# DeltaNet and an MLP in one kernel: chunk 0's inverse on four quadrants, and an instruction order worked back from deadlines

## The chip, the cores and the metric

The kernel runs on one core of a Trainium2 chip. The metric is the device time of one execution in microseconds; before the change it is 635.73 us, the median of three runs (632.64 to 637.24). The profiled execution has a span of 635.3 us. TensorE (PE) multiplies, VectorE (DVE), ScalarE (ACT) and GpSimd (POOL) do elementwise work, and SyncE (SP), ScalarE and GpSimd issue transfers.

## What is computed

There are 4 batches of 8 heads, 768 positions, head dimension 48. The attention is a delta rule with a state per head:

```
state = 0                                   # (48, 48) for each batch and head
for t in range(768):
    y[t]  = q[t] @ state
    v_old = k_n[t] @ state                  # k_n = k / (|k| + 1e-6)
    state = state + beta[t] * outer(k_n[t], v[t] - v_old)
```

The heads are put side by side to rows of 384, and a feed-forward block follows on each row:

```
xn  = (x - mean) / sqrt(var + 1e-6) * g_ln
out = x + relu(xn @ w_ch1) @ w_ch2          # 384 -> 1536 -> 384
```

All data is float32.

## The kernel before

**Chunks.** The 768 positions are cut into 12 chunks of 64 (C = 64). Within a chunk the recurrence is a triangular system: the matrix G holds the products of keys with each other, scaled by beta and the norms; X is the inverse of the unit triangular matrix; U = X (v - K S) gives the updates; the output is y = Q S + (masked Q K) U; and the state becomes S + K^T U. `recur(c)` holds these steps, layer norm and the transposes to the MLP's input `xnt`; `mlp(c)` holds the 12 first-layer steps (L1238, one for each 128 hidden columns, each three matmuls of 128x256) and 2 x 12 second-layer steps (L1254, 128x384 each) of a chunk's 256 rows. A matmul of float32 shows as two records in the profile. 32 (batch, head) pairs are stacked as two halves of 64 partitions (`half(e)`, e = 0 or 1) by 16 heads on the free axis; `GH` is 16, and groups g = 0 and 1 of 8 heads each are treated in turn.

**Three ways to the inverse.** From chunk 2 on, two chunks at a time form a slab: `prep_g` makes their G, stores it to DRAM and reloads it so that each partition has one 32x32 block, `rows_inverse` inverts it in 31 steps of two VectorE operations (L973, L978), the blocks go back through DRAM, and `join` puts the 64x64 inverse together with products E (L1037) and Z (L1042). Chunk 1 does the same with 16x16 blocks, 15 steps and two joins. Chunk 0 can't wait so long: `first_inverse` doubles the inverse on TensorE in levels n = 1 to 5. A level masks G (L816, on VectorE for n = 1 and 2, on GpSimd otherwise), multiplies it with the transposed inverse so far (E, L835), copies the result (L838), multiplies with a widened copy of the inverse (Z, L857 and L855), and writes back the inverse (L872) and its transpose (L873); `widen` (L807) makes the copy with both 32-column blocks. In these products both operands and the result of head (e, h) lie in the same half e. Only the tiles at rows 0, columns 0 and rows 64, columns 64 of the array are used. In the other attention products (`recur`, `products` for queries) odd heads have their result in the other half: `e ^ hp`, with hp the parity of the head, so all four 64x64 tiles work in turn.

**Weights.** w_ch1 and w_ch2 arrive as 12 pieces of 768 KB (`fetch`) into five buffers, two of which lie in `h_all`, and are converted with two ScalarE, three VectorE and one GpSimd operation a piece (`convert`: L633, L638, L643, L648, L653, L665).

**What sets the order.** Nothing runs in the order of the program text. Every operation is recorded as a `Step` with an engine, an assumed cost, its dependences and a priority `pr`; `Line.run` plays these forward with its own assumed times and picks, on each engine, the ready step with the lowest `pr`. `Line.emit` then issues all steps in that order, and `in_this_order` pins it, so each engine works through a fixed list. In the kernel before, `pr` was written by hand: -100 for chunk 0's chain, 10 c and nearby for chunk c, 1000 + 10 c for MLP steps, which thus fill gaps. `hold` steps (those at -100 and less) make an engine wait for them a little rather than start something long.

Of the kernel before, what the change touches and what calls it, by code (L numbers as in the profile page):

```python
# [16 lines left out]
C = 64  # L17
# [42 lines left out]
class Step:  # L60
    __slots__ = (
        "eng", "cost", "fn", "deps", "pr", "lag", "bulk", "start", "end", "n", "users", "name", "t0", "np", "arr", "hold", "ready"
# [3 lines left out]
class Line:  # L66
# [3 lines left out]
    HOP, GIVE = 0.17, 0.1  # L70
    PE_TAIL = 0.12
# [9 lines left out]
    def add(self, eng, cost, fn, r=(), w=(), pr=0.0, lag=0.0, bulk=None, name="", t0=0.7, after=(), np=0, arr=0.0, hold=None):  # L81
        s = Step()
        s.eng, s.cost, s.fn, s.pr, s.lag, s.bulk, s.name, s.t0 = eng, cost, fn, pr, lag, bulk, name, t0
        s.np, s.arr, s.n = np, arr, len(self.steps)
        s.hold = pr <= -100 if hold is None else hold
        deps = set()
        for k in r:
            if k in self.writer:
                deps.add(self.writer[k])
        for k in (*w, *after):  # L90
            if k in self.writer:
                deps.add(self.writer[k])
            deps.update(self.readers.get(k, ()))
        for k in r:
            self.readers.setdefault(k, []).append(s)
        for k in w:
            self.writer[k] = s
            self.readers[k] = []
        deps.discard(s)
        s.deps = sorted(deps, key=lambda d: d.n)  # L100
        s.start = s.end = None
        self.steps.append(s)
        return s
# [6 lines left out]
    def pe_time(self, s, t, commit):  # L110
        passes, bi, begun, wins = self.passes, self.block, self.begun, self.wins
        left, stall, new = max(s.np, 1), 0.0, {}
# [20 lines left out]
        if commit:  # L133
            self.passes, self.block, self.begun = passes, bi, begun
# [48 lines left out]
    def foresee(self, now):  # L183

        soon, ends = {e: [] for e in ENGS}, {}
        for s in self.held:
# [4 lines left out]
            t = max(s.t0, now)  # L191
# [7 lines left out]
    def run(self):  # L199
# [3 lines left out]
        self.passes, self.block, self.begun, self.wins = 0, 0, 0.7, {}  # L203
        self.avail = {e: [] for e in ENGS}
# [19 lines left out]
        while todo:  # L224
# [26 lines left out]
            if e == "PE" and len(now) > 1 and pick.pr >= 0 and pick.pr < 900:  # L251
                z, stall = self.pe_time(pick, t, False)
                if stall > 0.25:
                    for s in now:
                        if s.pr >= 900 and self.pe_time(s, t, False)[1] < 0.05:
                            pick = s
                            break
            first = [r for r, h in self.soon[e] if h.start is None and h.pr < pick.pr and t < r]
            if first and t + pick.cost > first[0] + self.GIVE and waits.get(e, 0) < 4:
# [3 lines left out]
                else:  # L263
                    waits[e] = waits.get(e, 0) + 1
# [28 lines left out]
    def schedule(self):  # L293
# [4 lines left out]
        for s in self.steps:  # L298
            s.users = users[s]
        self.run()  # L300
# [7 lines left out]
def kernel(  # L308
# [81 lines left out]
    bm = [sb(f"bm{i}", [128, 2]) for i in range(2)]  # L390
# [13 lines left out]
    dsw = sb("dsw", [128, GH])  # L404
# [52 lines left out]
    c_dve(lambda: nc.vector.memset(nought[:, 0:640], 0.0), 0.45, [("esx", 0), ("esx", 1)], pr=-300)  # L457
# [16 lines left out]
    for i in range(2):  # L474
        for b in range(2):
            c_dve(
                lambda i=i, b=b: nc.vector.tensor_scalar(
                    out=bm[i][:, b : b + 1], in0=xb[:, 0, 0:1].bitcast(I32), scalar1=b ^ i, scalar2=None, op0=ALU.is_equal
                ),
                0.15, [("bm", i, b)], ["bma"], pr=-99,  # L480
            )
# [16 lines left out]
    MPR = [-200, -99, -98, -98, -98, -98, -30]  # L498
    for n in range(7):
# [20 lines left out]
    MASK_SCRATCH = [(x, n) for x in ("ma", "mb") for n in range(7)] + ["bma", "eyx"]  # L520
    xc = us.rearrange("p h d -> p (h d)")[:, 0 : GH * BK].rearrange("p (h t) -> p h t", t=BK)
    c_pool(
        lambda: nc.gpsimd.tensor_copy(out=xc, in_=eye[:, None, :].to_broadcast([128, GH, BK])),
        0.62, [("xc", 0), ("xc", 1)], ["eye"],
# [20 lines left out]
    def load_first(engs, **kw):  # L545
        for g in range(2):
            for e in range(2):
                dma(
                    engs[e], tb[0].rearrange("p (h d) -> p h d", d=DP)[half(e), g * H : g * H + H, 0:D],
                    k[2 * e + g, :, 0:C, :].rearrange("h p d -> p h d"), H * C, 16.5, [], [("tb", 0, e, g)], **kw,  # L550
                )
# [22 lines left out]
    def load_blocks(i, src, c, eng, **kw):  # L574
        dst = tb[i].rearrange("p (h u d) -> p h u d", u=2, d=BK)
        for hp in range(2):
            for m in range(2):
                w = min(BK, D - BK * m)
                p0 = DP * hp + BK * m
                for u in range(2):  # L580
# [5 lines left out]
                        after=[("tb", i, e, g) for e in range(2) for g in range(2)], **kw,  # L586
                    )

    def tb_keys(i, kind):
# [3 lines left out]
        return [("tb", i, e, kind) for e in range(2)] + [("tbpad", i)]  # L593


    ON_DVE = (1, 2)
    BIG, SMALL, LEV = 2, 0, 0
# [78 lines left out]
    def fill(n, cols, size=128, behind=None, **kw):  # L676

        def go():
            for _ in range(n):
                nc.tensor.matmul(ffb[0:size, 1, 0:cols], nought[0:size, 512 : 512 + size], nought[0:size, 0:cols])  # L680
        t = max(PASS, cols * 0.845e-3) * 2 * n
        f = add("PE", t, go, [("esx", 0), ("esx", 1)], [FF2[0]], np=2 * n, arr=2 * n * cols * 0.845e-3 * (size / 128) ** 2, name="fill", **kw)
        if behind:
            f.deps.append(behind)
# [17 lines left out]
    def first_beta(ps, pk, **kw):  # L702
        def turn():
            for e in range(2):
                nc.tensor.matmul(ps[half(e), 0:GH], brow[BK * e : BK * e + GH, 0:C], ident[BK * e : BK * e + GH, BK * e : BK * e + GH])
        add("PE", 0.1, turn, [("brow", e) for e in range(2)] + ["ident"], pk, np=4, arr=0.02, **kw)
        add("DVE", 0.2, lambda: nc.vector.tensor_copy(out=bnat, in_=ps[:, 0:GH]), pk, ["bnat"], **kw)
# [21 lines left out]
    def first_swaps(**kw):  # L729
        add("ACT", 0.22, lambda: nc.scalar.mul(dsw[:, 0::2], ndb[:, 0::2], -1.0), [("nd", 0), ("nd", 1)], [("ds", 0)], **kw)  # L730
        for e in range(2):
            add(
                "ACT", 0.22, lambda e=e: nc.scalar.mul(dsw[half(1 - e), 1::2], ndb[half(e), 1::2], -1.0),
                [("nd", 0), ("nd", 1)], [("ds", 1 + e)], **kw,
# [24 lines left out]
    GM = [None, (gsbs[2], "g", 2), (gsbs[3], "g", 3), (xts[2], "xt", 2), (xts[3], "xt", 3), (gsbs[2], "g", 2)]  # L759
# [5 lines left out]
    def first_inverse(p_gk, gk, p_e, ek, p_x, xk, fill=None, **kw):  # L765

        gs, xt = gsbs[0], xts[0]
        pe_ = p_e.rearrange("p n (h t) -> p n h t", t=BK)
        px = [p_x[:, g, 0 : H * BK].rearrange("p (h t) -> p h t", t=BK) for g in range(2)]
        p_g = p_gk.rearrange("p n (j t) -> p n j t", t=C)  # L770
        shape = [128, H, 2, BK]
        kw0 = kw
        for g in range(2):
# [11 lines left out]
            for b in range(2):  # L785
# [4 lines left out]
                        xc[:, s], masks[0][:, None, cols].to_broadcast([128, H, BK]), gs[:, s, cols]  # L790
                    ),
                    [("g", 0, g), ("mask", 0)], [("xc", g)], **kw,
                )
            add("DVE", 0.45, lambda s=s: nc.vector.transpose(xnj[:, s], xc[:, s]), [("xc", g)], [("xn", g)], **kw)
            pe(
                2, lambda s=s, g=g: nc.tensor.matmul(px[g], ident, xnj[:, s], start=True, stop=True, skip_group_check=True),
                ["ident", ("xn", g)], xk[g], 0.43, **kw,
            )
# [3 lines left out]
        def widen(g):  # L802

            for b in range(2):
                o = spread(xt)[:, heads2[g], b]
                add(
                    "ACT", act(256), lambda o=o, b=b: nc.scalar.mul(o, xc[:, heads2[g]], bm[0][:, b : b + 1]),  # L807
                    [("xc", g), ("bm", 0, b)], [("xt", 0, g, b)], **kw,
                )

        def mask(n, g):
            gm, mk, s = GM[n][0], GM[n][1:], heads2[g]
            eng = ("DVE", nc.vector, dve(512)) if n in ON_DVE else ("Pool", nc.gpsimd, 0.3 + 1.95e-3 * 512)
# [8 lines left out]
        for n in range(1, 6):  # L822
            gm, mk = GM[n][0], GM[n][1:]
            last = n == 5
            for g in range(2):
                mask(n, g)
                if not last:
                    widen(g)
            for g in range(2):
                s = heads2[g]  # L830

                def prod_e(g=g, gm=gm):
                    for h in range(g * H, g * H + H):
                        for e in range(2):
                            nc.tensor.matmul(pe_[half(e), 0, h], gm[half(e), h], xnj[half(e), h])  # L835
                pe(32, prod_e, [mk + (g,), ("xn", g)], [ek[g]], 0.22, name=f"E{n}", **kw)
                if not last:
                    add("ACT", act(256), lambda s=s: nc.scalar.copy(es[:, s], pe_[:, 0, s]), [ek[g]], [("es", g)], **kw)  # L838
                    continue
                add(  # L840
                    "DVE", dve(512),
                    lambda s=s: nc.vector.tensor_tensor(
                        out=spread(esx)[:, s], in0=pe_[:, 0, s, None, :].to_broadcast(shape),
                        in1=bm[1][:, None, :, None].to_broadcast(shape), op=ALU.mult,
                    ),
                    [ek[g]] + [("bm", 1, b) for b in range(2)], [("esx", g)], **kw,
                )
            for g in range(2):
                s = heads2[g]

                def prod_z(g=g, last=last):
                    for h in range(g * H, g * H + H):
                        for e in range(2):
                            if last:
# [563 lines left out]
```

## Time and profile before

| What | Before |
|---|---|
| time, median of three | 635.73 us |
| TensorE busy, share of the span | 583.6 us, 92% |
| VectorE, ScalarE, GpSimd busy | 313.5, 172.0, 123.1 us |
| first product of chunk 0's inverse | 15.9 us |
| U of chunk 0 (second group) | 63.0 us |
| first MLP matmul | 81.1 us |
| first row step of slab 1 | 128.3 us |
| first join product of chunk 2 | 188.2 us |

A line of a timeline has the start, the duration of the group, engine, line, operation, output and inputs, shape and count, and in brackets how long the engine was idle before it and what ended that. A line of busy time by stage has the stretch, its length, busy time and count of instructions of each engine, the mean TensorE clock that was granted, the share of DMA and GB/s.

### The profile page before, as it was taken

To read this page: it belongs to the slowest core of one execution; us is meant where nothing else is said; L and a number is where in the kernel's file an instruction comes from. 1 tells how busy PE (TensorE), PEld (TensorE's weight loads), DVE (VectorE), ACT (ScalarE), POOL (GpSimd) and SP (SyncE) were. 2 spreads that over 40 slices of the span, in tenths; PEclk is the share of its full clock that TensorE was granted. 3 is DMA by queue.
4 is the path that set the end of the run, shared out by engine and by line. 5 is a ranking of instruction groups with operands and counts; after the bars stand their busy time and mean duration, and the time that the engine had idled before them with its cause. 6 is when DMAs were issued, how large, how long until landed. Compare 5 with 4: busy or idle time off the path is not lost.

```text
span 635.3 us, 20372 instructions
## 1 busy us (share of the span) xinstructions
PE 583.6 (92%) x9108; PEld 438.0 (69%) x9108; DVE 313.5 (49%) x711; ACT 172.0 (27%) x395; POOL 123.1 (19%) x163
## 2 busy tenths in 40 slices
PE   7887697568899989999999999999999999999996
PEld 5777675345677766866776867868767767777673
DVE  6345899367802589224784137871339812320000
ACT  5337375011221331223220331302322212222010
POOL 5264653711420224001340000010010100100000
PEclk9555689758799999999999999999999998999999
DMA  9921558873452563315815146103241040010101
GB/s 195 244 42 17 151 175 196 122 111 56 83 100 49 140 92 51 92 28 118 135 23 100 23 120 102 34 35 59 53 103 27 1 92 4 2 26 1 25 1 25
DMA packets 159975, 48.49 MB, mean 76 GB/s; under 512 B 151048, under 2 KB 154256, under 8 KB 159888
## 3 DMA queue, kind: packets, MB, share of 16 engines
q1 hardware_dynamic: 154032, 42.65, 32.6%
q0 software_dynamic: 2720, 3.96, 3.6%
q8 instruction: 71, 1.16, 0.8%
q10 hardware_dynamic: 3136, 0.59, 0.7%
q14 instruction: 16, 0.13, 0.1%
HBM read 33.93 MB, written 13.24 MB: 74 GB/s over the span
## 4 chain that ended last, share of the span: by engine, by line
PE 77%; DVE 9%; ACT 4%; SPq 3%; DMA 3%; issue 2%; DVEq 0%; ACTq 0%
PE ffa L1254 19%; PE ffa L1238 18%; PE ffb L1254 10%; PE ffb L1238 8%; SPq L441 3%; PE by L857 2%; PE two L835 2%; PE ffb L1042 2%; PE ffb L1037 2%; PE two L902 2%; PE two L1157 2%; PE by L1147 2%; PE two L1087 1%; PE by L1208 1%; PE two L1140 1%
## 5 line engine op out<-in xcount | busy, mean ns | idle before, releaser
L1238 PE MATMUL ffa<-xnt,w_sb 128*128 128x256 f32 x600 | 148.6, 394 | 5.8 <-ACT h_all L1246 3.7
L1254 PE MATMUL ffa<-w_sb,h_all 128*128 128x384 f32 x384 | 144.7, 495 | 1.2 <-ACT h_all L1246 1.1
L1238 PEld LDWEIGHTS ffa<-xnt,w_sb 128*128 128x128 f32 x600 | 113.6, 194 | 29.3 <-ACT h_all L1246 8.0
L1254 PEld LDWEIGHTS ffa<-w_sb,h_all 128*128 128x128 f32 x384 | 70.0, 190 | 46.0 <-ACT h_all L1246 4.0
L1254 PE MATMUL ffb<-w_sb,h_all 128*128 128x384 f32 x192 | 82.7, 517 | 5.3 <-DVE xt L1052 2.4
L1246 ACT ACTIVATE h_all<-ffa 128x256 f32<-128x256 f32 x100 | 35.0, 382 | 144.0 <-PE ffa L1238 103.5
L1238 PE MATMUL ffb<-xnt,w_sb 128*128 128x256 f32 x264 | 65.0, 382 | 0.2 <-DVE o L1263 0.2
L978 DVE TENSOR_TENSOR xb<-xb,tmp 128x60 f32<-128x60 f32 (+19 forms) x170 | 61.2, 360 | 5.8
L973 DVE TENSOR_TENSOR tmp<-xb,gb 128x60 f32<-128x60 f32 (+19 forms) x170 | 59.9, 352 | 3.3
L1072 POOL TENSOR_SCALAR knrm<-knrm 128x16 f32<-128x16 f32 x11 | 3.3, 297 | 275.9 <-ACT knrm L1068 275.9
L1238 PEld LDWEIGHTS ffb<-xnt,w_sb 128*128 128x128 f32 x264 | 49.5, 190 | 8.6 <-DVE o L1263 0.3
L1254 PEld LDWEIGHTS ffb<-w_sb,h_all 128*128 128x128 f32 x192 | 35.5, 196 | 28.6 <-DVE xt L1052 4.8
L441 POOL DMA_DIRECT2D tb<-in_k_dram x80 | 52.5, 663 | 11.2 <-DVE kt L886 10.7
L1052 DVE COPY xt<-ffb 32x512 f32<-32x512 f32 x22 | 15.0, 684 | 62.5 <-PE ffb L1037 28.5
L1246 ACT ACTIVATE h_all<-ffb 128x256 f32<-128x256 f32 x44 | 16.9, 384 | 76.7 <-PE ffb L1238 59.1
L1263 DVE TENSOR_TENSOR o<-ffa,x 128x384 f32<-128x384 f32 x16 | 8.7, 555 | 45.0 <-PE ffa L1254 43.7
L1030 DVE STREAM_TRANSPOSE xnj<-xt 128x512 f32<-128x512 f32 x11 | 7.8, 709 | 44.1 <-PE ffb L1037 23.8
L1263 DVE TENSOR_TENSOR o<-ffb,x 128x384 f32<-128x384 f32 x8 | 4.4, 555 | 40.7 <-PE ffb L1254 40.6
L653 POOL TENSOR_TENSOR words<-words,x 128x768 f32<-128x768 f32 (+1 forms) x11 | 20.1, 1828 | 22.7 <-DVE tmp L973 8.5
L1047 ACT ACTIVATE es<-ffb 32x512 f32<-32x512 f32 x22 | 13.0, 589 | 37.8 <-PE ffb L1254 15.2
L1064 DVE TENSOR_REDUCE ksum<-xln 128x16 f32<-128x768 f32 x11 | 10.5, 952 | 23.1 <-ACT xln L1063 23.0
L1181 ACT COPY x<-by 128x384 f32<-128x384 f32 x24 | 10.3, 482 | 36.3 <-PE by L1147 36.3
(161 smaller groups left out, 688.9 us busy)
## 6 DMA issues: line engine op xcount, KB each, us to landing
words<-in_moe_w_ch_dram SPq DMA_DIRECT2D x10, 768.0 KB, 5.2
gd<-gsb SPq DMA_DIRECT2D x11, 512.0 KB, 3.2
v<-in_v_dram SPq DMA_DIRECT2D x24, 192.0 KB, 4.3
kr<-in_k_dram SPq DMA_DIRECT2D x48, 96.0 KB, 3.6
out_dram<-o SPq DMA_DIRECT2D x48, 96.0 KB, 2.2
tb<-in_k_dram POOLq DMA_DIRECT2D x40, 64.0 KB, 3.1
gb<-gd SPq DMA_DIRECT2D x40, 64.0 KB, 3.6
tb<-in_q_dram SPq DMA_DIRECT2D x40, 64.0 KB, 2.8
```

The costliest lines, as they stand in the source:

```text
L441: add(eng, cost, lambda: QUEUE[eng].dma_start(out=out_, in_=in_), r, w, bulk=n * ns / 16e3, **kw)
L653: lambda: nc.gpsimd.tensor_tensor(out=lo.bitcast(FP32), in0=lo.bitcast(FP32), in1=esc.bitcast(FP32), op=ALU.mult),
L835: nc.tensor.matmul(pe_[half(e), 0, h], gm[half(e), h], xnj[half(e), h])
L857: nc.tensor.matmul(px[g][half(e), h - g * H], xt[half(e), h], es[half(e), h], start=False, stop=True, skip_group_check=True,)
L973: nc.vector.tensor_tensor(out=t, in0=xv[:, 0:n, j : j + 1].to_broadcast([128, n, w]), in1=gv[:, j : j + 1, j + 1 : L].to_broadcast([128, n ...
L978: nc.vector.tensor_tensor(out=rest, in0=rest, in1=t, op=ALU.subtract)
L1047: add("ACT", act(512), lambda rows=rows: nc.scalar.mul(es[rows], p[rows], -1.0), [ATT[1]], [("es", e)], **kw)
L1052: "DVE", dve(512), lambda rows=rows: nc.vector.tensor_copy(out=xt[rows, :, BK:C], in_=p[rows]),
L1238: nc.tensor.matmul(p[:, 0:TOK], w1_sb[:, t, f * 128 : (f + 1) * 128], xnt[:, t], start=(t == 0), stop=(t == KC - 1))
L1246: "ACT", act(256), lambda hk=hk, p=p: nc.scalar.activation(h_all[:, hk], p[:, 0:TOK], ACTF.Relu),
L1254: lambda f=f, g=g, p=p, hk=hs[f]: nc.tensor.matmul(p[:, 0:DM], h_all[:, hk, g * 128 : (g + 1) * 128], w2_sb[:, f], start=(f == 0), stop=(f ...
L1263: lambda o=o, p=p, g=g: nc.vector.tensor_tensor(out=o, in0=p[:, 0:DM], in1=x[:, g], op=ALU.add),
```

## The change

It has three parts.

**1. Chunk 0's inverse on four quadrants.** The keys are loaded so that odd heads of half e lie in half 1 - e (`load_first`; 8 loads in place of 4), and E and Z use row half `e ^ hp` and result half e (or the reverse for Z). The running inverse that is one factor of Z must then be in the half of its result, so `odd_back` copies it with three ScalarE operations a group: the even heads straight, the odd heads from one half into the other. E's result goes to the widened factor `esx` directly, one 32-column block on ScalarE (L880) and one on VectorE (L885), so `widen` and one copy a level go. Level 5 is done as in `join`, with 32x32 products (L906, L911). Masks: only level 1 of group 1 stays on VectorE, seven go to GpSimd. The norms move with the odd heads (`knat` in place of `dsw`).

**2. Priorities from deadlines.** Each MLP step gets a `due`: 42.0 + 42.2 c + 1.35 t, less 14 for c > 0. `schedule` goes through the steps backwards and sets `pr` to the latest end that still lets every user keep its own; hand-written priorities no longer count, except that steps nothing waits for get a large one. The steps that the first MLP step needs are laid out alone first, then all together, with the early ones not before their first time (`least`) and the tight ones on `hold`.

**3. Bunching.** On TensorE, once an MLP step is under way, MLP steps go on while one is ready, unless a small step is within 6 (URGENT) of its latest time; and small steps go on once one is under way. The order assumes 0.1 (SWITCH) for each change between the two kinds.

As built, TensorE's list has 153 changes between MLP and other steps where it had 165 (127 and 141 after the first join of chunk 2), 11 second-layer steps of MLP(1) stand before that join where 8 stood, and VectorE's row steps of chunk 1 follow at once on chunk 0's U. Three filler matmuls stand at the start in place of two.

The diff, cut to its core:

```diff
+    HOP, GIVE, PATIENCE, SLACK, EAGER = 0.17, 0.1, 1.5, 3.0, 0.0
+    URGENT, STALL = 6.0, 0.25
+    PE_TAIL, SWITCH = 0.12, 0.1
...
+            if e == "PE":
+                big = [s for s in now if s.due is not None]
+                small = [s for s in now if s.due is None]
+                if big and small:
+                    pick = big[0]
+                    if not self.big or small[0].pr - t < self.URGENT:
+                        fit = [s for s in small if self.pe_time(s, t, False)[1] < self.STALL]
+                        if fit:
+                            pick = fit[0]
+                        elif small[0].pr < t:
+                            pick = small[0]
...
+        for s in reversed(every):
+            took = s.cost if s.bulk is None else s.cost + self.DMA_ISSUE + self.DMA_DONE + 2 * s.bulk
+            took = max(took, 0.031 * s.np if s.due is None else 0.0)
+            late = [u.pr - took - (0.03 if u.eng == s.eng else self.HOP) for u in users[s]]
+            s.pr = min(late + [s.due if s.due is not None else 1e6])
...
+                    engs[e], tb[0].rearrange("p (h d) -> p h d", d=DP)[half(e ^ hp), g * H + hp : g * H + H : 2, 0:D],
+                    k[2 * e + g, hp::2, 0:C, :].rearrange("h p d -> p h d"), NP * C, 16.5, [],
...
-    ON_DVE = (1, 2)
-    BIG, SMALL, LEV = 2, 0, 0
+    ON_DVE = ((1, 1),)
+    BIG = 3
...
+    def odd_back(g, out_, in_, r, w, eng, **kw):
+        s = heads2[g]
+        for n in range(3):
+            hs = slice(s.start + (n > 0), s.stop, 2)
+            po, pi = (slice(0, 128),) * 2 if not n else (half(n - 1), half(2 - n))
+            src = in_[pi, int(n > 0)]
...
-                    for h in range(g * H, g * H + H):
-                        for e in range(2):
-                            nc.tensor.matmul(pe_[half(e), 0, h], gm[half(e), h], xnj[half(e), h])
+                    for h, hp, j, e in order[g]:
+                        a = half(e ^ hp)
+                        nc.tensor.matmul(pe_[half(e), 2 * g, hp, j], gm[a, h], xnj[a, h])
...
+                    for h, hp, j, e in order[g]:
+                        nc.tensor.matmul(
+                            px[g][half(e ^ hp), hp, j], esx[half(e), h], xc[half(e), h],
+                            start=False, stop=True, skip_group_check=True,
+                        )
...
-    first_kt(0, 1, qts[0], ("qt", 0), two, TWO, pr=-94)
-    queries(0, ffb, ATT + FF2, pr=-100)
+    first_kt(0, 1, qts[0], ("qt", 0), ffb, ATT + FF2, pr=-99)
+    queries(0, ffb, ATT + FF2, halves=True, pr=-100)
...
+    def due(c, t):
+        return 42.0 + 42.2 * c + 1.35 * t - (14.0 if c else 0.0)
```

## Prediction

> **What bounds the kernel now.** I read the page's busy line and slices first, then the busy time by stage, then TensorE's and VectorE's timelines of the first 190 us.
>
> ```profile
> PE 583.6 (92%) x9108; PEld 438.0 (69%) x9108; DVE 313.5 (49%) x711; ACT 172.0 (27%) x395; POOL 123.1 (19%) x163
> PE   7887697568899989999999999999999999999996
> PEclk9555689758799999999999999999999998999999
> ```
>
> 92% busy looks finished, but the clock row says otherwise: from slice 13 on TensorE is full at full clock; before it, it is half clocked or waiting. By stage (PE, weight load, DVE, ACT, POOL, clock, DMA):
>
> ```profile
> 0.00:15.90 15.90, 12.28 (x98) 8.31 (x98) 10.24 (x43) 7.98 (x15) 8.14 (x22) 1.00 1.07 195
> 15.90:63.00 47.10, 38.35 (x675) 35.97 (x676) 20.78 (x47) 22.92 (x53) 20.63 (x25) 0.51 0.46 102
> 63.00:81.10 18.10, 12.47 (x367) 11.21 (x367) 15.69 (x26) 6.05 (x12) 11.14 (x11) 0.59 0.52 135
> 81.10:118.20 37.10, 32.50 (x352) 22.70 (x352) 31.64 (x60) 18.95 (x32) 19.81 (x15) 0.94 0.72 177
> 118.20:188.20 70.00, 53.13 (x952) 38.60 (x954) 39.11 (x91) 10.69 (x27) 23.00 (x35) 0.76 0.61 97
> 188.20:635.30 447.10, 434.90 (x6669) 321.16 (x6668) 196.03 (x448) 105.39 (x258) 40.38 (x57) 1.00 0.27 55
> ```
>
> The last row is the bound stage: 434.9 of 447.1 us busy, 5 of the idle 12 us the final store. It can hardly shrink. The 188 us before it hold MLP(0) (31 us when full: 12 x 1.30 + 24 x 0.65 by the starts of L1238 and L1254), two thirds of MLP(1) and attention of two chunks; the rest is lost. Chunk 0's inverse, on TensorE:
>
> ```profile
> 31.96 1.92 PE L835 MATMUL two<-xnj,xt 64*64 64x32 f32 x32 [0.23 <-ACT xnj L872]
> 34.40 3.62 PE L857 MATMUL by<-es,xt 64*64 64x32 f32 x64 [0.52 <-ACT es L838]
> 39.14 3.63 PE L835 MATMUL two<-xnj,xt 64*64 64x32 f32 x64 [1.12 <-ACT xnj L872]
> ...
> 62.99 1.11 PE L1121 MATMUL two<-v,xt 64*64 64x48 f32 x32 [1.22 <-DVE u L1127]
> 63.85 1.98 PE L902 MATMUL ffb<-kt 48*64 48x64 f32 x64
> 65.58 1.94 PE L1157 MATMUL two<-u,kr 64*64 64x48 f32 x64
> ```
>
> 32 records of the two-quadrant kind take 1.73 us from start to start, 54 ns each; 64 of the four-quadrant kind (L902, L1157) also take 1.7 us, 27 ns each, at the same half clock. Then the chain waits on VectorE:
>
> ```profile
> 124.94 1.93 PE L1005 MATMUL ffb<-xnj,gsb 32*32 32x32 f32 x128 [7.42 <-DVE xnj L999]
> ...
> 188.16 1.20 PE L1037 MATMUL ffb<-xnj,gsb 32*32 32x32 f32 x64
> ```
> ```profile
> 31.28 0.97 DVE L515 SCALAR_TENSOR_TENSOR m<-xb 128x64 f32<-128x64 int32 x1
> 32.18 1.25 DVE L1283 TENSOR_SCALAR scale_w<-g_sb 128x3 f32<-128x3 f32 x1
> ```
> ```profile
> 30.91 2.50 POOL L816 TENSOR_TENSOR xt<-gsb,m 128x512 f32<-128x512 f32 x2 [6.21 <-DVE m L515]
> ```
>
> 188.16 is E(2), chunk 2's first join: the marker I forecast by. The last three lines: VectorE operations of 0.2 us take 1 us while GpSimd runs 1.25 us ones.
>
> **What the skill says.** "TensorEngine Tiling (Array Packing)", Tiling Modes: 64x64 gives four tiles that work independently, and changing the mode drains the engine. The trace agrees on both: 54 against 27 ns above, and in the steady stage two L1254 pairs between small steps take 1.48 us (206.48 to 207.96) where they need 1.29, so 0.095 us for an edge. "TensorE: Matmul & The Clock Gate", Part 1: the clock is halved until a window of activity; the trace has 0.51 in the inverse although TensorE was 81% busy there[...]. "SBUF — State Buffer", Who interferes with whom: a VectorE operation with two SBUF inputs or in a two-port mode and a GpSimd operation lock each other out; agreed, lines above. "ScalarE: Activation LUTs", What ACT_TABLE_LOAD costs: back-to-back activations overlap by about 93 ns; here two 0.37 us copies take 0.65.
>
> **Start, to 16 us.** Chunk 0's keys come in eight loads instead of four; three issues take 2.35 us, so each queue is 1.4 us later with the second group and everything behind it. Against that, the first product E1 waited 1.16 us for the query transposes in the same bank, and these move to another bank and later. The shorter memset saves 0.4 us of VectorE before the first filler; the third filler (0.9 us) lies in the wait for keys; the removed mask, the beta and norm edits are 0.2 us operations, hidden while the keys load. Seven of eight group masks now run on GpSimd (1.27 us each, L816), one after the other from 12.7 us, when VectorE's predicated copies (0.45 us) want the lock. The trace of before does not show a predicated copy against GpSimd. Unlocked: E1 at 14.5 and 16 us for the two groups; every copy held to the next GpSimd boundary: 16 and 19. I take the latter.
>
> **Inverse, 16 to 63 us.** Per group and level: E 32 x 27 ns = 0.87, 0.19 to its end, 0.47 to the next product (as E to Z shows today: the copy and the hops; ScalarE and VectorE now take one half each), Z 0.87 + 0.19, transpose and hops 0.55 (L873: 0.45): 3.15 us. The two groups interleave, TensorE has 3.5 us for both. Four levels from 19: 31.6. The last level (32x32 tiles, 30 ns a record by L1037): 1.05 + 0.5 + 1.05 + 0.5 = 3.1, so 34.7. Added on ScalarE: 30 copies of 128 columns that bring odd heads back; no row of the trace has them, between the 64x8 operations (0.22) and the 256-column copy (0.37), so 0.27 less 0.09 overlap: 5.5 us. With some 30 others (evictions, conversions at 0.55 to 0.65) ScalarE has 18 to 20 us of work in these 19, so it paces the chain: 2.5 us more (0 to 5). U starts at 37.5 and not at 57.9 and 63: **25 us**. If the doubled density warms the clock, 5 us less.
>
> **U to MLP(0), 18 us today (62.99 to 81.07).** The queries of chunk 0 and their mask come before U, so the 3.36 us that L1147 waited for pt go. U 1.7, u on VectorE 1.1, y 1.7, x copy 0.9, then layer norm between row pairs of chunk 1 in VectorE's order 5.4, transposes and copy 1: 11.8. MLP(0) at 49.
>
> **VectorE to slab 1's rows.** Chunk 1's rows (15 pairs of about 0.42, 6.3 us) now stand right behind U, and nine weight pieces follow: 0.56 + 0.55 + 1.01 (L638, L643, L665) = 2.1 each, 19 us; 13 us of others (two pt/kt rounds, layer norm, reduce, v, join, norms of slab 1). From 38 that is 76 without a wait. GpSimd's nine products (1.85 each, 17 us) lock a part of it, 5 us: 81. The fetch says the same: three buffers, about 12 us from issue to release (5.2 landing, then 0.9 + 0.55 + 0.55 + 1.0 + 1.85 + 1.0), 4 us a piece, last seven from 50: 78 to 80. Before, rows of slab 1 began at 128.3.
>
> **Rows to E(2).** 31 pairs take 22.5 us (0.19 to 0.42 an operation), work that stands between them 16 us, waits 3: 123; store, reload and transpose took 7.1 (175.36 to 182.44): 130 to 131. TensorE's own path: 49 + 54 (31.2 of MLP(0), 22.8 of MLP(1): 12 first and 11 second steps) + 24 (some 23 small steps) = 127 and a few us of waits for weights. Both meet near **132**, against 188.2.
>
> **Steady stage.** 447.1, less three second-layer steps already done (2.0), less 14 of 141 mode edges (1.3 us): 443.8. The second layer's two banks alternating cost nothing: 0.645 us a step either way (from 243.9). "qs" only fixes an order on TensorE. Bunching puts the waits of small steps behind MLP steps as today; I claim none of the 7 us of idle. Sum: 132 + 443.8 = **576 us**.
>
> **Rivals.**
> - Warm inverse, no lock: U at 31, E(2) at 122: 566. For it, 64 to 69 us warmed to 0.65 with four quadrants; against, those had no gaps. 0.12.
> - Locks and weight fetch hold slab 1's rows to 92 and E(2) to 147: 591. For it, today conversions and rows spread over 74 us, with single operations of 1.8 to 2.2 us. 0.17.
> - Only chunk 0 shortens and each later stage keeps its length: E(2) at 163, 606. Against it, VectorE idles 10 us in 112 to 125 and the row order did change. 0.11.
> - Slower: bunching uncovers each chunk's chain of v (0.95), u (0.80), state (0.95), layer norm (2) and hops, 5.5 us; over 11 chunks 60 us, 576 + 60 = 636 and more, 640. Against it, MLP steps still stand between nearly all of them. 0.05.
> - The forecast: 0.55.
>
> **Numbers.** 558 to 602 leaves out the last two and a little of the tails. Faster 0.94, same 0.01, slower 0.05.
>
> **What would show it.** Right: E and Z at about 27 ns a record, U near 37, the first MLP matmul near 49, slab 1's rows near 81, E(2) near 132, then about 444 us at clock 1.0. Wrong: records still at 54 ns; predicated copies not held (a gain) or ScalarE gaps above 1 us before each Z (a loss); TensorE idle between 60 and 130 with VectorE or the weight queue as releaser; idle of more than 12 us after E(2).

## The result and the profile after

The changed kernel takes 607.18 us (median of 4 runs, 605.44 to 608.59) where the kernel before takes 634.18 (632.26 to 637.24): a ratio of 0.957, 95% interval 0.952 to 0.962. It is 27 us faster; the forecast was 58 us, a time of 576 in a range of 558 to 602, so the time lies outside it. The busy line and the first rows of the slices of the changed kernel's page:

```profile
PE 556.4 (92%) x9118; PEld 414.8 (68%) x9118; DVE 315.0 (52%) x709; ACT 171.9 (28%) x406; POOL 125.0 (21%) x164
...
PE   7855886999999999799989899998999999999996
...
PEclk9555697999999999999999999999999999999999
```

The clock row is at 9 from slice 8 on, where before it was so from slice 12 (but for one 8 near the end). TensorE is busy 27 us less. Some 11 us of that lie in the inverse: from the first E to the first group's U it was busy 35.3 us before and is busy 24.0 now. By stage, cut at the first E, the first group's U, the first MLP step, slab 1's rows and E(2). The stages of before in the prediction are cut at the second group's U (63.0) and at 118.2 us, so their rows don't pair off one by one with these; the table of marks below compares like with like. The columns are PE, weight load, DVE, ACT, POOL, clock, DMA share, GB/s:

```profile
15.45:53.00 37.55, 23.95 (x719) 21.58 (x718) 27.61 (x51) 21.80 (x58) 25.70 (x30) 0.50 0.81 176
53.00:68.30 15.30, 9.53 (x207) 8.10 (x207) 12.42 (x41) 7.53 (x14) 4.50 (x4) 0.50 0.02 3
68.30:106.10 37.80, 30.07 (x756) 24.41 (x758) 30.95 (x40) 19.85 (x34) 19.88 (x14) 0.88 0.78 198
106.10:156.30 50.20, 49.46 (x630) 35.09 (x625) 35.63 (x85) 9.30 (x24) 22.28 (x35) 1.00 0.79 131
156.30:606.50 450.20, 431.61 (x6663) 317.98 (x6662) 196.84 (x448) 104.45 (x258) 40.78 (x58) 1.00 0.27 55
```

The first row is the disappointment: the inverse takes 37.5 us where the forecast had 21.5, with TensorE 64% busy and no engine full. From the rows to E(2) TensorE is busy 49.5 of 50.2 us. The marks of all kernels, in us from the start of the span, read off TensorE's and VectorE's timelines (the experiments follow below; U is that of the first head group, and the second group's follows it: 63.0 before, 54.6 in the changed kernel; "rest" is from E(2) to the end). A kernel's executions can lie 1.5% and more above its fastest, and as e10's profiled one does, e10 has no row here:

| kernel | first E | first U | MLP(0) | slab 1's rows | E(2) | span | rest |
|---|---|---|---|---|---|---|---|
| forecast | 16 | 37.5 | 49 | 81 | 132 | 576 | 443.8 |
| before | 15.9 | 57.9 | 81.1 | 128.3 | 188.2 | 635.3 | 447.1 |
| changed | 15.5 | 53.0 | 68.3 | 106.2 | 156.3 | 606.5 | 450.2 |
| e1 conversions later | 15.5 | 47.3 | 76.6 | 118.6 | 168.7 | 616.1 | 447.4 |
| e2 GpSimd later | 15.5 | 51.7 | 67.0 | 102.3 | 153.3 | 603.5 | 450.2 |
| e3 new inverse, old order | 14.6 | 48.1 | 69.3 | 110.5 | 167.7 | 618.0 | 450.3 |
| e4 old inverse, new order | 16.1 | 58.3 | 100.9 | 125.8 | 173.9 | 620.7 | 446.8 |
| e6 = e1, E split | 15.0 | 45.6 | 74.2 | 118.7 | 168.8 | 618.5 | 449.7 |
| e7 = e1, X split | 15.4 | 45.0 | 74.5 | 116.3 | 166.2 | 617.2 | 451.0 |
| e8 = e1, both split | 19.9 | 51.8 | 78.4 | 132.3 | 173.6 | 623.5 | 449.9 |
| e9 = e2, X split | 15.0 | 49.0 | 64.3 | 99.4 | 152.0 | 602.1 | 450.1 |
| e11 = e9, wide conversions later | 14.9 | 46.9 | 68.6 | 105.9 | 160.0 | 606.7 | 446.7 |
| e12 = e9, products on VectorE | 15.1 | 47.7 | 62.1 | 105.6 | 154.9 | 602.5 | 447.6 |

### The profile page after: what moved, and what is told of

It reads as the page before. It is cut to its first block, busy times and chain, and to the rows that moved or that the text cites. A ratio compares the mean times of both kernels' runs of the same rounds, so it can differ in the third digit from the quotient of the medians.

```text
span 606.5 us, 20389 instructions
## 1 busy us (share of the span) xinstructions
PE 556.4 (92%) x9118; PEld 414.8 (68%) x9118; DVE 315.0 (52%) x709; ACT 171.9 (28%) x406; POOL 125.0 (21%) x164
## 4 chain that ended last, share of the span: by engine, by line
PE 77%; DVE 11%; ACT 4%; issue 3%; DMA 3%; SPq 2%; ACTq 0%; DVEq 0%
PE ffa L1294 20%; PE ffa L1310 18%; PE ffb L1310 10%; PE ffb L1294 9%; PE two L950 3%; SPq L475 2%; PE ffb L1094 2%; PE by L1199 2%; DVE tmp L1025 2%; DVE xb L1030 2%; PE ffb L1089 2%; PE by L1139 2%; PE two L1192 2%; PE two L1209 1%; PE by L1261 1%
## 5 line engine op out<-in xcount | busy, mean ns | idle before, releaser
L1310 PE MATMUL ffb<-w_sb,h_all 128*128 128x384 f32 x192 | 79.2, 494 | 4.7 <-ACT es L1099 2.8
L1025 DVE TENSOR_TENSOR tmp<-xb,gb 128x60 f32<-128x60 f32 (+19 forms) x170 | 58.3, 343 | 4.0
L1082 DVE STREAM_TRANSPOSE xnj<-xt 128x512 f32<-128x512 f32 x11 | 7.8, 710 | 49.8 <-DMA xt<-xd 28.3
L1319 DVE TENSOR_TENSOR o<-ffa,x 128x384 f32<-128x384 f32 x16 | 8.8, 556 | 41.7 <-PE ffa L1310 37.0
L1319 DVE TENSOR_TENSOR o<-ffb,x 128x384 f32<-128x384 f32 x8 | 4.4, 552 | 41.2 <-PE ffb L1310 35.3
L933 DVE STREAM_TRANSPOSE qt<-tb 128x1024 f32<-128x1024 f32 x10 | 12.4, 1240 | 16.5 <-PE two L950 16.5
```

Of the source, the lines that this page charges most:

```text
L933: lambda: nc.vector.transpose(dst.rearrange("p i (u t) -> p i u t", t=BK), tb[i].rearrange("p (h u d) -> p h u d", u=2, d=BK)),
L1025: nc.vector.tensor_tensor(out=t, in0=xv[:, 0:n, j : j + 1].to_broadcast([128, n, w]), in1=gv[:, j : j + 1, j + 1 : L].to_broadcast([128, n ...
L1310: lambda f=f, g=g, p=p, hk=hs[f]: nc.tensor.matmul(p[:, 0:DM], h_all[:, hk, g * 128 : (g + 1) * 128], w2_sb[:, f], start=(f == 0), stop=(f ...
L1319: lambda o=o, p=p, g=g: nc.vector.tensor_tensor(out=o, in0=p[:, 0:DM], in1=x[:, g], op=ALU.add),
```

## The experiments

The first four ask where the inverse loses its time, and which half of the change brings what. Theories: A, weight conversions stand ahead of the chain's operations in the engines' in-order queues; B, the products or ScalarE's copies are slower than forecast; C, GpSimd's work in the inverse holds VectorE. What suggested A and C, in the changed kernel's timeline of all engines (start, duration, engine, line):

```profile
42.15 3.12 DVE L673 TENSOR_SCALAR words<-words 128x768 uint32<-128x768 uint32 x1
...
42.99 1.86 POOL L1379 MEMSET xt<- 128x1024 f32 x2
44.77 3.45 POOL L475 DMA_DIRECT2D tb<-in_k_dram  x5
45.19 0.43 DVE L898 STREAM_TRANSPOSE xnj<-by 128x256 f32<-128x256 f32 x1
...
46.03 1.08 PE L893 MATMUL by<-u,pt 64*64 64x32 f32 x32 [2.74 <-ACT u L811]
```

A conversion of 768 columns (0.56 us elsewhere) takes 3.12 us while GpSimd clears two buffers and issues loads; the transpose of X waits behind it, and TensorE behind the copies that follow it.

**e1, conversions later**, on VectorE, ScalarE and GpSimd alike.

```
-            convert(i, c0, 384, pr=-50 if c0 == 0 else -10)
+            convert(i, c0, 384, pr=-50 if c0 == 0 else -10, t0=36.0)
-        convert(i, pr=2)
+        convert(i, pr=2, t0=36.0)
```

> The changed kernel, with all weight conversions moved behind chunk 0's inverse in the list of every engine (an earliest start of 36 for them in the planner). Theory A, the conversions that stand between the chain's steps on VectorE and GpSimd hold the inverse: from the first E to the first U it takes 24 us or less instead of 37.5, U starts near 40, TensorE's waits above 1 us in the inverse go; the conversions then follow U, so the first MLP matmul gains less than U does and the time is 595 to 607. Theory B, the four-quadrant products and the three copies back on ScalarE are slow by themselves: first E to first U stays above 32 us, time 605 to 620. Theory C, GpSimd's memsets and DMA issues lock VectorE out: 30 to 34 us, the masks and v scale gone or not.

Measured: 617.81 us (617.05 to 619.99), 0.972 of before [0.968, 0.976]. First E to U took 31.8 us and not 37.5, so A is right for 5.8 us of the inverse and no more: it expected 24 us or less and 595 to 607 in all. The work then came back: U to MLP(0) took 29.3 us and not 15.3. Conversions have to be done before MLP(0), and the inverse was not the worst place for them. But 31.8 us is still 10 more than forecast, with VectorE busy 11.7 and ScalarE 14.8 of them. That is the trace to look at, because no weight conversion is left in this stretch (GpSimd's loads and memsets still are).

**e2, GpSimd's memsets and block loads later** (the loads for chunks 2 and 3 and the clearing of two X buffers).

```
-            load_blocks(2 * (c % 2), k, c, "Pool", pr=pr, t0=40.0 * m if m > 1 else 18.0)
+            load_blocks(2 * (c % 2), k, c, "Pool", pr=pr, t0=40.0 * m if m > 1 else 36.0)
-            "Pool", 1.0, lambda i=i: nc.gpsimd.memset(xts[i], 0.0), [], [("xz", i)], pr=20,
+            "Pool", 1.0, lambda i=i: nc.gpsimd.memset(xts[i], 0.0), [], [("xz", i)], pr=20, t0=36.0,
```

> The changed kernel, with GpSimd's key loads and the two memsets of xt moved behind the inverse, conversions left where they are. Theory C: the 3.12 and 2.25 us operations of VectorE (L673) become short, first E to first U falls from 37.5 to 30 us or less, time 598 to 602. Theory A: only the one wait of 2.7 us goes, first E to first U 34 to 36 us, and the later key loads give part of it back: time 603 to 612. Theory B: no change in the inverse at all.

Measured: 604.75 us (604.15 to 606.42), 0.952 [0.947, 0.956]. The same conversion takes 0.55 us now (43.48 us in e2), so C is right that GpSimd's work made it long. But first E to U still takes 36.2 us, and not C's 30 or less, and the time is in A's range: every mark from U on is 1 to 4 us earlier, so C is there but small. The interval touches that of the changed kernel.

**e3 and e4, one half of the change each.** e3 is the changed kernel with the planner of before, e4 the kernel before with the new planner and due times. One of the many places that e3 changes:

```
...
-                due=due(c, 1.3 * f), np=6, arr=1.3,
+                pr=1000 + 10 * c, np=6, arr=1.3,
...
```

> Part 1 alone: the new inverse with the planner of before (hand-written priorities, MLP steps last, no deadlines, no bunching). Theory A: the gain of 27 us belongs to the inverse and to row steps that follow at once; here the inverse takes some 30 us, U starts near 48, and the time is 610 to 620. Rival, the order does it: 625 to 635, with the inverse short but slab 1's rows still at 115 us or later.

> Parts 2 and 3 alone: the old inverse on two quadrants, with deadlines and bunching. If the parts add, this plus part 1 alone gives 27 us; Theory A expects 622 to 632 here, as the chain of 47 us stays and only the rows of slab 1 come earlier. Rival, the order does it: 610 to 618.

Measured: e3 621.79 us (619.01 to 625.09), 0.978 [0.973, 0.984]; e4 621.77 us (619.65 to 622.46), 0.977 [0.973, 0.981]. The two products, 0.978 x 0.977 = 0.956, are the whole change: each half brings 13 us, and they add up. Both times lie just outside what A expected (610 to 620 for e3, 622 to 632 for e4), on the side of its rival, but nearer to A. The marks show where each works: the new inverse brings U to 48.1 and the rows to 110.5 with the old order (the second group's U comes at 53.4, against 54.6 in the changed kernel); the new order shortens the stretch from rows to E(2), 59.9 us before and 57.2 in e3, to 48.1 in e4 and 50.1 in the changed kernel, since MLP steps now fill it.

**A new theory from e1's trace.** One level of e1's inverse, all engines; the two head groups alternate, and the bracket says what each waited for:

```profile
28.46 1.08 PE L876 MATMUL two<-xnj,xt 64*64 64x32 f32 x32 [0.66 <-DVE xnj L898]
...
29.86 1.38 PE L876 MATMUL two<-xnj,xt 64*64 64x32 f32 x32 [0.33 <-DVE xnj L898]
...
31.31 0.47 ACT L880 ACTIVATE pt<-two,bm 128x256 f32<-128x256 f32 x1 [0.73 <-PE two L876]
...
31.81 0.42 DVE L885 TENSOR_TENSOR pt<-two,bm 128x256 f32<-128x256 f32 x1 [2.10 <-ACT pt L880]
32.27 0.47 ACT L880 ACTIVATE pt<-two,bm 128x256 f32<-128x256 f32 x1 [0.49 <-DVE pt L885]
...
32.29 2.05 PE L893 MATMUL by<-u,pt 64*64 64x32 f32 x64 [1.05 <-DVE pt L885]
32.78 0.42 DVE L885 TENSOR_TENSOR pt<-two,bm 128x256 f32<-128x256 f32 x1 [0.54 <-ACT pt L880]
...
34.41 0.45 DVE L898 STREAM_TRANSPOSE xnj<-by 128x256 f32<-128x256 f32 x1 [1.20 <-PE by L893]
34.95 0.83 ACT L811 COPY u<-by 128x128 f32<-128x128 f32 x3 [2.20 <-DVE xnj L898]
...
35.01 1.08 PE L876 MATMUL two<-xnj,xt 64*64 64x32 f32 x32 [0.67 <-DVE xnj L898]
35.81 0.45 DVE L898 STREAM_TRANSPOSE xnj<-by 128x256 f32<-128x256 f32 x1 [0.95 <-ACT u L811]
```

The first group's E ends at 29.5, but its copy by ScalarE starts at 31.31, after the second group's E. VectorE's half of that copy starts when ScalarE's has ended, ScalarE's copy for the second group when VectorE's has, and so on to the end of the level: every access to `two`, and then every access to `by`, waits for the one before it, of whichever group and engine. Each of the two tiles is two banks of PSUM, and both groups lie in the same two. So this is theory D: **the shared tiles make the two groups' steps wait for each other**, and a level takes 6.2 to 6.6 us. "PSUM — Partial Sum Buffer" of the Trainium skill says why a program must do so, under "PSUM bank collisions raise a hardware error": no two of TensorE, ScalarE and VectorE may be in one bank and quadrant at once, two readers included, and semaphores therefore guard by bank and quadrant, not by address. The trace agrees, by the waits above: two copies of 0.47 and 0.42 us out of the same banks never overlap. Rival B remains: that copies and hops take this long by themselves. e6, e7 and e8 give the groups tiles of their own, all on e1, where no conversion stands in the queues. They move a sum to another tile and so to other banks at once, so they can't tell which of the two counts; e5 below can.

**e6, the second group's E in ffa.**

```
-        pe_ = p_e.rearrange("p n (z j t) -> p z n j t", z=2 * 2, t=BK)
+        pe_ = [x.rearrange("p n (z j t) -> p z n j t", z=2 * 2, t=BK) for x in (p_e, ffa)]
...
+        ek = [ek[0], FFA[1], ek[2], FFA[3]]
...
```

> As the kernel with late weight conversions (617.8 us), in whose inverse VectorE and ScalarE are mostly idle and a level still takes 6.2 to 6.5 us, but the second head group's E products lie in ffa, no longer in the two banks of the first group's. Theory D (accesses of different engines to one bank go one after the other, so the two groups can't interleave): the copy of the first group's E no longer waits for the second group's E, nor for its copies; it then stands behind ScalarE's copies of X, so 0.7 us a level, first E to U from 31.8 to 29 or 30. Rival B (ScalarE's copies and the hops themselves pace): no change, 31.5 to 32. Total 615 to 618 for D, 617 to 619 for B, as the later VectorE work sets the rest.

**e7, the second group's X in ffa.**

```
-        px = [p_x[:, :, g * NP * BK : (g + 1) * NP * BK].rearrange(...) for g in range(2)]
+        px = [x[:, :, g * NP * BK : (g + 1) * NP * BK].rearrange(...) for g, x in enumerate((p_x, ffa))]
...
```

> As the kernel with late weight conversions, but the second group's X is summed in ffa, the first's in by. Theory D: the transpose of the first group's X no longer waits for the second group's Z (0.95 us), the second's no longer for the first's three copies (0.9): 1.4 us a level from the second level on, first E to U from 31.8 to 27 or 28. Rival B: no change, 31.5 to 32. Total 613 to 616 for D, 617 to 619 for B.

**e8, all four apart** (E in two and ffb, X in by and ffa; query transposes behind level 2, query products behind the inverse).

> As the kernel with late weight conversions, with all four products in tiles of their own (E in two and ffb, X in by and ffa); chunk 0's query transposes go behind level 2, its query products behind the inverse, which may cost 1 to 2 us. Theory D: what is left in a level is one group's own chain, 1.06 + 0.17 + 0.47 + 0.45 + 0.17 + 1.06 + 0.17 + 0.45 + 0.17 = 4.2 us, with the other group beside it: levels 3 and 4 take 4.2 to 4.8 us and not 6.2 to 6.5, first E to the first U 24 to 27 us and not 31.8. Rival B: 6 us or more a level, 31 to 33. Total 610 to 615 for D, 617 to 620 for B.

Measured: e6 618.11 us (615.27 to 620.21), e7 616.75 (615.46 to 618.88), e8 622.47 (618.56 to 625.18). From the starts of E in levels 3, 4 and the last, e1 takes 6.55 and 6.20 us a level, e6 5.74 and 5.64 (28.48, 34.22, 39.86), e7 6.82 and 5.03 (27.45, 34.27, 39.30). In e7's first of these two, TensorE stood still for 1.77 us in the middle of the second group's E with no wait in the trace, and why stays open. First E to U took 31.8 us in e1, 30.6 in e6 and 29.6 in e7. For e8, TensorE's timeline, the first group's E and Z:

```profile
26.95 1.08 PE L877 MATMUL two<-xnj,gsb 64*64 64x32 f32 x32
...
29.62 1.06 PE L894 MATMUL by<-u,pt 64*64 64x32 f32 x32
...
31.33 1.08 PE L877 MATMUL two<-xnj,xt 64*64 64x32 f32 x32
...
38.16 1.09 PE L877 MATMUL two<-xnj,xt 64*64 64x32 f32 x32
...
42.33 0.65 PE L909 MATMUL two<-xnj,gsb 32*32 32x32 f32 x32
```

26.95 to 31.33 is 4.38 us and 38.16 to 42.33 is 4.17, as D expected; the second group's two levels take 4.40 (26.08 to 30.48) and 4.00 (37.32 to 41.32). The level between holds the query transposes and takes 6.8 us. On the levels D is right and B is not: e6 and e7 change the place of one sum each and save some 0.7 and 1.3 us a level, and with all sums apart a level fell from 6.2 to 6.6 to 4.2 to 4.4. e8 also moves chunk 0's query steps, but e1's levels 3 and 4 hold none of these, so the comparison of these levels is not touched by it. On the whole inverse and on the time D was too hopeful: it expected first E to U in 29 to 30, 27 to 28 and 24 to 27 us. e8 took 32.0, which is B's figure, because its first level took 7.1 us, the one with the transposes 6.8, and the second group's last product waited 4.5 us for ScalarE; of the totals, e6's 618.1 doesn't tell D from B, and e7's and e8's stay above D's ranges (613 to 616, 610 to 615). As a kernel e8 is no gain either: the first E starts only at 19.9, behind a changed order of the first steps (TensorE waits 3.1 us for L754).

**Back to a faster kernel.** e9 and e10 split X or E on e2, where conversions stay in the inverse.

> The kernel with GpSimd's memsets and block loads later (604.75 us; U 51.7, slab 1's rows 102.3, E(2) 153.3), and the second group's X in ffa. If shared banks still matter while conversions stand in the queue: U at 48 to 50, 600 to 603 in all. Rival: conversions and their waits hide it, U at 51 to 52 and 604 to 606.

> The same with the second group's E in ffa in place of its X. Shared banks: about half as much as for X, as with late conversions (0.7 us a level against 1.2): U at 49.5 to 51, 602 to 604. Rival: 604 to 606.

Measured: e9 599.76 us (597.56 to 603.86), 0.944 [0.941, 0.948]; e10 602.27 (596.17 to 605.75), 0.946 [0.941, 0.952]. Both stay below the changed kernel; e9's interval lies wholly below the changed kernel's. U came at 49.0 in e9, 2.7 us earlier than in e2, and the whole kernel gained 5.0 by the medians: shared tiles count with full queues too. e10's time is as expected.

**e11 and e12, what holds VectorE behind U.** e11 moves two conversions of full width behind the inverse (`convert(i, pr=2, t0=36.0 if i in (3, 4) else 0.7)`), e12 puts GpSimd's product of the last six pieces on VectorE (`nc.vector if i > 5 else nc.gpsimd`), both on e9.

> As the split of X with GpSimd's work later, and the two conversions of full width (pieces 3 and 4, with VectorE operations of 768 columns, up to 3.12 us in the inverse) behind the inverse too; the halves of pieces 0 to 2 stay in it. If what counts for the end is the inverse: U at 44 to 46 and 597 to 601. If the work of conversion only comes back behind U, as with all six pieces late: U at 44 to 46 but slab 1's rows no earlier than 102 and 603 to 608.

> As the split of X with GpSimd's work later, and the product of pieces 6 to 11 on VectorE (0.9 us each) and not on GpSimd (1.85 us each, behind other work of its queue). In the changed kernel VectorE is busy 43.4 of the 53.1 us from U to slab 1's rows, as forecast, and idle 9.7. If that idle time is the chain of a piece through GpSimd: U to rows 44 to 47 us and not 50.6, 596 to 600 in all. Rival (the transfer of the words sets the pace): U to rows 49 to 51, 601 to 605.

Measured: e11 607.95 us (606.29 to 612.37), 0.960; U at 46.9 (44 to 46 was expected) but rows at 105.9, so the work only comes back, as in e1. e12 601.71 us (600.63 to 604.19), 0.949 [0.946, 0.953], no better than e9; U to rows 57.9 us. The theory of the chain through GpSimd fell: without GpSimd's products VectorE still idled 11.4 us of these 57.9, 5.1 of them for ScalarE's first step of a piece (L668), the step right behind the transfer. The rival's total is right, its 49 to 51 us for the stretch is not, and what set the 57.9 is not settled.

**e5, e13, e14, the stretch after E(2).** In the changed kernel the waits of this stretch that grew most are those of MLP steps into ffb for a join's copies out of ffb's other bank (columns: engine, tile and line that waited, what for, us in total, times, longest):

```profile
PE ffb L1310 <- ACT es L1099: 2.8, 3, 1.4
PE ffb L1310 <- DVE xt L1104: 1.6, 2, 0.8
...
PE ffb L1294 <- ACT es L1099: 1.4, 1, 1.4
```

In the kernel before they sum to 1.6 us, here to 5.8. Next to them, MLP steps into ffa wait 2.9 us for VectorE's L1319, where it was 0.2. Theory F says that two banks of one tile are made to wait for each other; rival G that the matter is one of too few banks. e5 takes ffb from the MLP (`fbanks[turns[1] % 2]`), e13 the joins from ffb (`p = (by if c > 1 else ffb)[:, 0]`), e14 does that on e9.

> The MLP's sums rotate over the two banks of ffa alone, never in ffb, the tile of the joins. After the changed kernel's E(2) TensorE is busy 431.6 us and idle 18.6, and 5.8 us of the idle time are MLP steps into ffb that wait for ScalarE's or VectorE's copy of a join out of ffb's other bank (L1310 and L1294 ffb, by L1099 and L1104). Theory F (two banks of one tile are made to wait for each other, and the bunches put MLP steps right behind a join): these waits vanish, the stretch after E(2) is 444 to 446 us, the time 601 to 603. Rival G (the idle time is a matter of two banks for twelve steps, of evictions): with two banks and not three the waits for ScalarE's h_all grow by as much or more, 450 to 456 after E(2), 607 to 613 in all.

> The joins of chunks 2 and up sum in by and not in ffb; the MLP keeps its three banks, one of them in ffb. The list on TensorE has 121 edges between MLP steps and small steps, and not 153, which by 0.095 us an edge is 3 us of busy time. Theory F (MLP steps wait for copies out of the other bank of the same tile): the waits of ffb steps for L1099 and L1104 go from 5.8 us to under 1, the stretch after E(2) from 450.2 to 442 to 445 us, all in all 598 to 602. Rival G (TensorE merely waits for the joins' copies wherever they lie, or by with its other uses is no better): other waits of 4 us or more come up, 447 us or more after E(2), 604 to 608.

> The same with GpSimd's work later and the second group's X in ffa (599.8 us without the joins' move, 450.1 after E(2)). Theory F: 443 to 446 after E(2), 592 to 596. Rival G: 447 to 451 after E(2), 597 to 602.

Measured: e5 670.63 us (669.95 to 673.58), 1.059 [1.051, 1.067]; e13 646.86 (645.65 to 655.29), 1.022 [1.012, 1.032]; e14 657.40 (653.16 to 663.35), 1.035 [1.022, 1.048]. Both cures are far worse than the ill. e5's stretch after E(2) takes 501.8 us, and its waits say why:

```profile
PE ffa L1294 <- ACT h_all L1302: 24.4, 47, 0.9
PE ffa L1310 <- ACT h_all L1302: 9.6, 20, 0.5
```

67 MLP steps wait for the eviction of an earlier one, in all 34 us. Rival G named these waits, but expected 607 to 613 us, and its reason, two banks where there were three, is not what the trace shows: what the MLP lost with ffb is not only a bank but its second tile. Here two steps fill ffa's two banks one after the other, and then ScalarE empties both:

```profile
317.82 2.86 PE L1294 MATMUL ffa<-xnt,w_sb 128*128 128x256 f32 x12
320.71 0.66 ACT L1302 ACTIVATE h_all<-ffa 128x256 f32<-128x256 f32 x2 [3.12 <-PE ffa L1294]
```

A step is six records, so the first bank was full near 319.4, and ScalarE was idle. It started only at 320.71, when the second step had ended in the other bank. TensorE and the eviction thus take turns, and the second bank hides nothing. So it is throughout: each of the four PSUM tiles `two`, `by`, `ffa` and `ffb` is two banks, and in the traces of all these kernels no access of ScalarE or VectorE to one of them overlaps an access of another engine to the same one by more than 0.05 us, in 6108 accesses that were compared. In the changed kernel 333 of 385 such accesses do overlap with TensorE's work in another tile. **The waits go by the tile, not by the bank.** The page's rule asks for bank and quadrant, so the order seen in these traces is stricter than the rule. That is theory F's mechanism, and theory D's waits follow from it as well; there the two groups also lie in the same banks, so that the rule would ask for waits too.

In e13 the ffb waits are gone, but by, which the joins now share with the attention's other sums, makes the small steps wait instead (15 us in four rows of e13's waits); its stretch takes 500 us (e14's 496), of which these waits are the smaller part: TensorE is also busy 36 us more, at a mean clock of 0.95. Some 7 of the 36 are the 11 second-layer steps of MLP(1), which in e13 come behind E(2). Theory F is borne out in its mechanism, not as a way to gain. Whether the 4.2 us would go if the joins had a tile of their own was not tried, as all four PSUM tiles have other uses; nor were tiles of one bank each, so what they would bring is not shown.

## Why the prediction was wrong, step by step

**Start.** Right: E at 15.45 and 18.15 us against 16 and 19, with the predicated copies held by GpSimd as taken (the first pair took 2.33 us for 2 x 0.45).

**Inverse: the step that failed.** "The two groups interleave, TensorE has 3.5 us for both", and with it "3.15 us" a level and group. The rate was right: 32 records start in 0.87 us, 27 ns each, at clock 0.50. One group's chain was too short, 4.2 to 4.4 us with tiles of its own (e8), mostly since "ScalarE and VectorE now take one half each" took the two reads of one tile to go side by side; they go one after the other (31.31 and 31.81 in e1). Above all the groups do not interleave freely: they share tiles, and a level takes 6.2 to 6.6 us. The first group's four levels took 25.7 us in e1 (15.53 to 41.21) where the forecast had 12.6 for a group and 15.6 with the second group's later start; the last level and its copies took 6.1 against 5.9. That is 10 us: a level took 6.4 us on average where the sum has 3.15, and of the 3.3 too many some 1.1 are the chain that was too short (e8's level less 3.15) and 2.2 the shared tiles (e1's less e8's). Weight conversions in the engines' queues, of which the sum had only ScalarE's, are the other 5.8 (e1). Together they are 16 of the 30.5 us by which the span missed. (The working also adds 34.7 and 2.5 to 37.5; it is 37.2.)

The trace before already showed that the groups wait for each other. The prediction prints its line of E at 39.14, 3.63 us for both groups together, so the first group's half was done near 41. Yet ScalarE, idle, copied it only when the second group's had ended too:

```profile
42.86 0.37 ACT L838 COPY es<-two 128x256 f32<-128x256 f32 x1 [2.39 <-PE two L835]
```

The 2.5 us for ScalarE as the pacer is wrong: it had 21.8 us of work, little more than forecast, but was idle 16 us in the inverse, waiting for others.

**U to MLP(0).** 15.3 us against 11.5 in the forecast's marks, so 3.8 more: the second group's U is 1.6 us later than the first's, and two VectorE row operations of 0.2 us took 1.09 and 1.76 beside two GpSimd products, 3.66 us together (55.48).

**VectorE to slab 1's rows.** The work was right and the idle time wrong. U to rows has 43.4 us of VectorE's work, just the 43 forecast, locks included; the forecast said "without a wait", and 9.7 us of idle time were added, 4.0 of it for ScalarE's first step on late pieces and 2.2 for GpSimd's products. e12 shows that GpSimd's products are not what to shorten.

**Rows to E(2).** The length is right, 50.1 us against 51, and half of the reason: two paths were to meet at E(2), and only TensorE's sets it. The joins' input was ready at 152.3 us (L1082), 4 us before E(2), and TensorE was busy 49.5 of 50.2 us. That the other path came out near it as well is partly luck.

**Steady stage.** Busy time fell from 434.9 to 431.6 us, exactly the 3.3 forecast, but "I claim none of the 7 us of idle" was too kind: idle time rose by 6.4 us, 4.2 of it the ffb waits and 2.7 the waits for L1319. The stretch takes 446.7 to 451.0 us in all twelve kernels of the table, which keep the joins and the MLP's third bank in ffb, in whatever order, so a few microseconds of it belong to no single edit.

Sum of the misses in the marks: -0.5 + 16.0 + 3.8 + 5.9 - 0.9 + 6.4 = 30.7: from the 575.8 to which the forecast's own terms add up, to the span of 606.5. Against the rounded 576 the span missed by 30.5. The profiled execution's time, 608.22 us, is 1.7 more than its span.

**The rivals.** "Locks and weight fetch" had the mechanism behind U but only part of it; "each later stage keeps its length", with 606 us, hit the number by luck: later stages did shorten, the inverse did not enough. The "Warm inverse" did not come, nor did the 5 us "If the doubled density warms the clock": the inverse ran at 0.50. The sign that was named for it, 0.65 at 64 to 69 us, is misread; the trace of before has 0.55 there, and 0.50 until 68. Bunching uncovered no chain of 5.5 us per chunk: e4, order alone, is 13 us faster.

## What to carry to other kernels

Before you let two groups of heads overlap, list which PSUM tile each step reads and writes. In this kernel accesses of different engines to one tile went one after the other, even in different banks of it, and two chains that were independent but for their tiles took 6.2 to 6.6 us a level where 4.2 to 4.4 is what one takes with tiles of its own. An in-order queue must be costed with everything that stands in it during the chain, not with the chain's own operations. And work moved out of a hole must have another hole: late conversions made the inverse 6 us shorter and the kernel 11 us slower.

## What was not expected of the hardware

- VectorE's tensor-scalar operation with one SBUF input, 128x768, took 3.12 us and not 0.56 beside GpSimd memsets and load issues (42.15 us in the changed kernel); with that work moved away, in e2, it took 0.55 (43.48). "SBUF — State Buffer" of the skill, under Who interferes with whom, lists it among operations that can enter a two-port mode and then lock; the trace agrees.
- The whole inverse ran at clock 0.50 although all four quadrants work and TensorE was busy 64% of it; in the kernel before it was 81% and 0.51. So idle quadrants alone don't explain a half clock; what kind of activity the clock counts, these runs don't tell.
